# A soft-capped attention with two feed-forward layers: VectorE's order within a pair of heads, the queue of the first queries, and the last copy

## The chip, the cores and the metric

The kernel runs on one core of a Trainium2 chip. A core has five engines with instruction queues of their own: TensorE (PE, with its weight loads shown as PEld), VectorE (DVE), ScalarE (ACT), GpSimd (POOL) and SyncE (SP), which here only starts transfers. They run in parallel and wait for each other through semaphores; within one engine the instructions go in the order in which they were issued. The metric is the device time of one execution in microseconds (us).

## The reference

Attention with a soft cap over 2 batches of 12 heads, 448 tokens and 64 dimensions; its result, laid out as 896 tokens by 768, goes through two feed-forward layers.

```python
scores = scale * np.matmul(q, k.transpose(0, 1, 3, 2))
scores = cap * np.tanh(scores / cap)
scores = scores - np.max(scores, axis=-1, keepdims=True)
attn = np.exp(scores)
attn = attn / (np.sum(attn, axis=-1, keepdims=True) + 1e-09)
x = np.matmul(attn, v)                      # -> 896 x 768
g = s * np.maximum(x @ w_in, 0.0) ** 2 + b  # w_in 768 x 2048
x = g @ w_out                               # 2048 x 768
h = x @ w2_in                               # 768 x 1024
solu = h * softmax(h)
ln = (solu - mean) / np.sqrt(var + 1e-06) * g_ln
out = ln @ w2_out                           # 1024 x 768
```

The weights of the layers are float64 and are converted on the chip.

## The kernel before

**Precision.** Most factors are split into a high and a low part, and a product is three matmuls (high by high, high by low, low by high).

**The attention** runs over 12 pairs of heads. For a pair n, scores are computed by key: TensorE makes four score tiles `s` (`scores_by_key`, L465), ScalarE takes the tanh of each (L470) and then the exponential of two stretches of the tile `e` (`exps_by_key`, L477). The sum over the keys goes through `sums_by_key`: GpSimd adds the first two key tiles of each head (L486, as soon as the first exponential is there), then the third (L489, after the second exponential), and VectorE adds the last piece with two instructions, one for each head (L492, the *last additions* of the sum `c`). Two pairs later TensorE multiplies `e` by the values (`products_by_key`, tile `o`, L504) and sums `c` over the partitions by a matmul with ones (`values_by_key`, tile `m`, L514). VectorE then normalises: a transpose of `m` (`mt`, L521), a reciprocal (`few`, L523), a transpose back (`rs`, L527) and the product `xf` (L532). GpSimd splits `xf` into high and low (`split_x`, L541 and L545), for the last two pairs ScalarE and VectorE do. Meanwhile the keys and queries of pair n+2 are transposed on TensorE (`pk`, `pq`, L423) and split by VectorE and ScalarE (`prep_half`, tiles `kh`, `kl`, `qh`, `ql`, L446, L447, L434 or L438, L439). In the same loop the first weights are converted piece by piece (`weights.pump`, L222 to L247: one instruction or a few in a pair).

**What sets the order.** In the loop over pairs, `then(step, ...)` chains each step behind the one before on TensorE, VectorE, ScalarE and GpSimd, so on each engine the order is the one written in the loop. In a pass n VectorE has: normalisation of n-2, splits of n+2, conversion, last additions of n. The tiles `o`, `m`, `pk` and `pq` share four PSUM banks (`ps_t`), the score tiles have two pairs of banks, `xf` has two buffers, `c` and `e` three.

**The start.** k and q of the first two pairs are loaded into buffers that later hold weights (`raw`, named `first["k"]` and `first["q"]`). SyncE and ScalarE issue the keys of the first pair and, behind them, one head's queries each (L147); GpSimd zeroes the unused parts of the key tiles (L94) and issues the queries of the second pair (L126).

**The end.** The last 128 rows of the result come in two column blocks (512 and 256 wide). Each is copied from PSUM in two halves, the first by ScalarE (L1036), the second by VectorE (L1037), and then stored.

**After the attention** TensorE runs through the two layers; the weights are loaded by SyncE and converted by ScalarE and VectorE ahead of their use.

Of the kernel before, what the change touches and what calls it, by code (L numbers as in the profile page):

```python
# [37 lines left out]
def tile_softcap_attention__relu2__solu(  # L38
# [15 lines left out]
    nc = tc.nc  # L54
# [5 lines left out]
    NC = 4  # L60
# [70 lines left out]
    first = {}  # L131
# [4 lines left out]
    nc.scalar.dma_start(out=cap_t, in_=cap.partition_broadcast(P))  # L136
    ident = cst.tile([P, P], F32, name="ident")
    make_identity(nc, ident)
    zero_by_key(first["k"], True)
    load_by_query(first["q"][:, 1:], q, 0, slice(2, 4), nc.gpsimd)  # L140
    for pr in range(2):
        pair = slice(2 * pr, 2 * pr + 2)
        odd = nc.scalar if pr == 0 else nc.sync
        load_by_key(first["k"][:, pr:pr + 1], k, 0, pair, by_pair=True, odd=odd)
        if pr == 0:
            for j, queue in enumerate((nc.sync, nc.scalar)):
                queue.dma_start(  # L147
                    out=first["q"][:, 0, :, j],
                    in_=q[0, j].rearrange("(p c) d -> p c d", c=NC),
                )  # L150
    s_t = cst.tile([P, 1], F32, name="s_t")
    b_t = cst.tile([P, 1], F32, name="b_t")
    a_t = cst.tile([P, 1], F32, name="a_t")
# [28 lines left out]
    def layers(ctx, general):  # L182
# [229 lines left out]
        st = {}  # L412
# [68 lines left out]
        def sums_by_key(n, half):  # L481
            e = st["e", n]
            if half == 0:
                c = ap_.tile([P, 2, S], F32, tag="c", name=f"c{n}", bufs=3)
                st["c", n] = c
                nc.gpsimd.tensor_tensor(out=c, in0=e[:, 0:2, :], in1=e[:, 2:4, :], op=ALU.add)  # L486
                return
            c = st["c", n]
            nc.gpsimd.tensor_tensor(out=c, in0=c, in1=e[:, 4:6, :], op=ALU.add)  # L489
            for j in range(2):  # L490
                r = slice(j * D, (j + 1) * D)
                nc.vector.scalar_tensor_tensor(  # L492
                    out=c[r, j, :], in0=c[r, j, :], scalar=1e-9 / D, in1=e[r, 6, :],
                    op0=ALU.add, op1=ALU.add,
                )
# [210 lines left out]
        NPR = NH // 2  # L706
# [8 lines left out]
        if general:  # L715
            load_group(2, ("v",))
            for n in range(NPR + 2):
                for c in range(NC):
                    i, c2 = 2 * n + c // 2, c % 2
                    if i < NH:  # L720
                        scores(i, c2)
                    if 0 <= i - 1 < NH:
                        exps(i - 1, c2)
                    if 0 <= i - 2 < NH:
                        transposes(i - 2, 2 * c2)
                        transposes(i - 2, 2 * c2 + 1)
                    if c < 2:
                        prep_half(n + 1)
                if n % 2 == 1 and n // 2 + 3 < NG:
                    load_group(n // 2 + 3)  # L730
                if n >= 2:
                    values(n - 2)
        else:
            last = {}
            traced = nc.cur_bb.bb.instructions

            def then(step, *args):
                with ExitStack() as behind:
                    for ins in last.values():
                        behind.enter_context(tc.issue_after(ins))  # L740
                    n = len(traced)
                    step(*args)
                for ins in traced[n:]:
                    if ins.engine in ordered:
                        last[ins.engine] = ins

            ordered = [e.engine for e in (nc.tensor, nc.vector, nc.scalar, nc.gpsimd)]
            xs["x"] = act_tiles("x")
            idle = ps_t.tile([P, 512], F32, tag="t", name="idle2")
            for n in range(6):  # L750
                nc.tensor.matmul(idle[:D, :D], lhsT=ones, rhs=ones, start=True, stop=True)
            then(scores_by_key, 0, 0)
            then(scores_by_key, 0, 1)
            then(prep_half, 1)
            then(prep_half, 1)
            weights.load(0)
            load_group(2, ("k", "q"))
            load_small()
            load_group(1, ("v",))
            load_group(2, ("v",))  # L760
            weights.load(1)
            steps = {1: 3, **{n: 1 for n in range(3, NPR - 2)}, NPR - 2: 2, NPR - 1: 3}
            for n in range(NPR + 2):
                now = n < NPR
                if now and n > 0:
                    then(scores_by_key, n, 0)
                    then(scores_by_key, n, 1)
                if not now:
                    then(weights.pump, 2)
                if n == 1:  # L770
                    then(prep_half, 2)
                    then(prep_half, 2)
                    then(sums_by_key, 0, 1)
                if n >= 2:
                    then(products_by_key, n - 2, 0)
                    then(products_by_key, n - 2, 1)
                    then(values_by_key, n - 2)
                if now:
                    then(exps_by_key, n, 0)
                if n >= NPR:  # L780
                    then(split_x, n - 2)
                elif n >= 3:
                    then(split_x, n - 3)
                if now:
                    then(sums_by_key, n, 0)
                    then(scores_by_key, n, 2)
                    then(scores_by_key, n, 3)
                    then(exps_by_key, n, 1)
                if n > 0:
                    then(prep_half, n + 2)  # L790
                    then(prep_half, n + 2)
                then(weights.pump, steps.get(n, 0))
                if now and n > 0:
                    then(sums_by_key, n, 1)
                if n == NPR - 1:
                    then(split_x, n - 2)
                if n % 2 == 1 and n // 2 + 3 < NG:
                    load_group(n // 2 + 3, ("k", "q"))
                if n % 2 == 1 and 3 <= (n + 3) // 2 < NG:
                    load_group((n + 3) // 2, ("v",))  # L800
# [203 lines left out]
        def out2(t):  # L1004
            ln = ln_of.pop(t)
            lh = fin2.tile([P, KF2, P], F32R, tag="lh", name=f"lh{t}", bufs=2)
            ll = fin2.tile([P, KF2, P], F32R, tag="ll", name=f"ll{t}", bufs=2)
            with tc.high_priority(offset=200):
                for n in range(2):
                    ps = ps_x.tile([P, 4, P], F32, tag="x", name=f"x{t}_{n}")  # L1010
                    for c in range(4):
                        nc.tensor.transpose(ps[:, c, :], ln[:, n, c * P:(c + 1) * P], ident)
                    split_evac(lh[:, 4 * n:4 * n + 4, :], ll[:, 4 * n:4 * n + 4, :], ps)
            last = t == NTT - 1
            cuts = (slice(0, 512), slice(512, DM)) if last else (slice(0, NO), slice(NO, DM))
            if t == NTT - 2:
                po = ps_h.tile([P, 2, 512], F32, tag="h", name=f"o{t}")
            else:
                po = ps_o.tile([P, 2, 512], F32, tag="o", name=f"o{t}")
            parts = [po[:, 0, :], po[:, 1, :]]  # L1020
            if last:
                parts[1] = ps_h.tile([P, 2, 512], F32, tag="h", name=f"o{t}b")[:, 0, :]
            ot = wt_tile(f"ot{t}")
            order = [(f, n) for f in range(KF2) for n in range(2)]
            if last:
                order.sort(key=lambda fn: fn[1])
            for f, n in order:
                m = cuts[n]
                o = parts[n][:, :m.stop - m.start]
                wh, wl = (w[:, m] for w in w2o_of[f])  # L1030
                nc.tensor.matmul(o, lhsT=lh[:, f, :], rhs=wh, start=(f == 0), stop=False)  # L1031
                nc.tensor.matmul(o, lhsT=lh[:, f, :], rhs=wl, start=False, stop=False)  # L1032
                nc.tensor.matmul(o, lhsT=ll[:, f, :], rhs=wh, start=False, stop=(f == KF2 - 1))  # L1033
                if last and f == KF2 - 1:
                    half = (m.start + m.stop) // 2
                    nc.scalar.copy(out=ot[:, m.start:half], in_=o[:, :half - m.start])  # L1036
                    nc.vector.tensor_copy(ot[:, half:m.stop], o[:, half - m.start:])  # L1037
                    store(ot, t, m)
            if not last:
                nc.scalar.copy(out=ot.rearrange("p (a m) -> p a m", a=2), in_=po[:, :, :NO])  # L1040
                store(ot, t, slice(0, DM))
# [70 lines left out]
```

## Time and profile before

| | |
|---|---|
| median of 3 runs | 475.89 us (475.87 to 476.15) |
| the profiled execution | 475.96 us, of which the span is 474.2 us |
| TensorE busy | 458.5 us (97%) |
| VectorE busy | 358.2 us (76%) |
| ScalarE busy | 273.1 us (58%) |
| GpSimd busy | 92.5 us (20%) |
| TensorE's granted clock | 0.999 of full speed |

The span is the time from the first to the last event of the trace; the profiled execution has 1.8 us around it. The attention takes the first 104 us or so. GpSimd's 92.5 us lie almost all in it, as do VectorE's busiest stretches; behind it VectorE is in reserve most of the time.

### The profile page before, as it was taken

The numbers are of one execution on the slowest core, as the hardware profiler recorded it, in microseconds if no ns is written. First come the engines' busy times: TensorE is split into PE (matmuls) and PEld (weight loads), VectorE is DVE, ScalarE is ACT, GpSimd is POOL, SyncE is SP. The second block draws the span as 40 slices with busy tenths as digits, with TensorE's granted clock in tenths as the row PEclk, the third lists the DMA queues.
The fourth block names the chain that finished last, engine by engine and source line by source line (L and its number), as shares of the span: only waits on it lengthen the run. The fifth ranks groups of instructions, "written<-read, shape, count | busy, mean of one in ns | idle before, by whom it ended". The sixth has DMA issues, their size and how long they took to land.

```text
span 474.2 us, 6582 instructions
## 1 busy us (share of the span) xinstructions
PE 458.5 (97%) x2432; PEld 378.1 (80%) x2432; DVE 358.2 (76%) x566; ACT 273.1 (58%) x394; POOL 92.5 (20%) x91
## 2 busy tenths in 40 slices
PE   7789999999999999999999999999999999999995
PEld 6545465546899898998988889898888898999894
DVE  2799999998798999995699988998959984043110
ACT  3978988781586766755677755555625453033120
POOL 8677777882000000000000000000001010000000
PEclk9999999999999999999999999999999999999999
DMA  7784460014435775532323224443412401011112
GB/s 146 169 198 99 111 180 1 12 56 133 156 115 177 223 218 177 157 117 82 90 80 99 88 91 133 134 133 134 133 68 68 132 1 33 2 33 35 35 45 62
DMA packets 45081, 49.28 MB, mean 104 GB/s; under 512 B 21808, under 2 KB 37296, under 8 KB 45040
## 3 DMA queue, kind: packets, MB, share of 16 engines
q1 hardware_dynamic: 43568, 47.85, 34.8%
q0 software_dynamic: 384, 0.69, 0.7%
q8 instruction: 21, 0.34, 0.3%
q10 hardware_dynamic: 1088, 0.23, 0.2%
q14 instruction: 20, 0.16, 0.1%
HBM read 46.01 MB, written 2.75 MB: 103 GB/s over the span
## 4 chain that ended last, share of the span: by engine, by line
PE 75%; DVE 16%; SPq 4%; DMA 2%; issue 1%; ACT 1%; ACTq 0%; DVEq 0%
PE y L333 8%; PE y L334 8%; PE y L332 8%; PE in L332 7%; PE in L333 7%; PE in L334 7%; DVE c L492 5%; PE h L982 4%; PE h L986 4%; PE h L990 4%; PE o L1032 4%; PE o L1033 4%; PE o L1031 4%; SPq L112 3%; PE o L504 1%
## 5 line engine op out<-in xcount | busy, mean ns | idle before, releaser
L333 PE MATMUL in<-xl,h_wi 128*128 128x510 f32 (+2 forms) x192 | 70.2, 366 | 0.0
L332 PE MATMUL in<-xh,h_wi 128*128 128x510 f32 (+2 forms) x192 | 69.9, 366 | 0.4 <-ACT xh L203 0.4
L334 PE MATMUL in<-xh,l_wi 128*128 128x510 f32 (+2 forms) x192 | 69.9, 365 | 0.0
L967 POOL TENSOR_SCALAR va<-vs 128x1 f32<-128x1 f32 x7 | 2.0, 288 | 321.9 <-ACT e L966 321.9
L364 ACT ACTIVATE gh<-g,s_t 128x510 fp32r<-128x510 f32 (+1 forms) x64 | 42.1, 667 | 18.8 <-PE y L334 18.8
L365 DVE SCALAR_TENSOR_TENSOR gl<-g,s_t,gh 128x510 fp32r<-128x510 f32 (+1 forms) x64 | 42.7, 682 | 3.0 <-ACT gh L364 2.8
L470 ACT ACTIVATE e<-s 128x896 f32<-128x896 f32 (+1 forms) x48 | 36.8, 818 | 11.3 <-PE s L465 11.2
L504 PE MATMUL o<-e,vn 128*64 128x448 f32 x192 | 39.0, 545 | 3.5 <-DVE mt L521 3.5
L477 ACT ACTIVATE e<-e,a_t 128x1792 f32<-128x1792 f32 (+1 forms) x24 | 40.7, 1698 | 0.8
L333 PEld LDWEIGHTS in<-xl,h_wi 128*128 128x128 f32 x192 | 36.0, 188 | 5.3 <-issue 1.4
L332 PEld LDWEIGHTS in<-xh,h_wi 128*128 128x128 f32 x192 | 35.9, 188 | 5.0 <-ACT xh L203 0.7
L334 PEld LDWEIGHTS in<-xh,l_wi 128*128 128x128 f32 x192 | 36.0, 188 | 4.3 <-issue 0.7
L1031 PE MATMUL o<-w2o_h,lh 128*128 128x384 f32 (+1 forms) x104 | 35.6, 342 | 0.5 <-ACT lh L203 0.5
L1033 PE MATMUL o<-w2o_h,ll 128*128 128x384 f32 (+1 forms) x104 | 35.4, 342 | 0.0
L1032 PE MATMUL o<-w2o_l,lh 128*128 128x384 f32 (+1 forms) x104 | 35.4, 340 | 0.0
L492 DVE SCALAR_TENSOR_TENSOR c<-c,e 64x448 f32<-64x448 f32 x24 | 33.1, 1377 | 0.4
L982 PE MATMUL h<-w2i_h,yh 128*128 128x512 f32 x84 | 33.0, 393 | 0.0
L986 PE MATMUL h<-w2i_l,yh 128*128 128x512 f32 x84 | 33.0, 392 | 0.0
L990 PE MATMUL h<-w2i_h,yl 128*128 128x512 f32 x84 | 32.8, 390 | 0.0
L504 PEld LDWEIGHTS o<-e,vn 128*64 128x64 f32 x192 | 13.7, 136 | 23.4 <-issue 16.8
L486 POOL TENSOR_TENSOR c<-e 128x896 f32<-128x896 f32 x12 | 28.9, 2406 | 5.7 <-ACT e L477 5.3
L489 POOL TENSOR_TENSOR c<-c,e 128x896 f32<-128x896 f32 x12 | 25.6, 2130 | 14.2 <-ACT e L477 14.2
(428 smaller groups left out, 1089.4 us busy)
## 6 DMA issues: line engine op xcount, KB each, us to landing
raw<-in_moe_w_in_dram SPq DMA_DIRECT2D x16, 768.0 KB, 4.9
raw<-in_moe_w_out_dram SPq DMA_DIRECT2D x24, 512.0 KB, 3.6
raw_w2i<-in_moe_w_in_dram SPq DMA_DIRECT2D x12, 512.0 KB, 3.7
raw<-in_moe_w_out_dram SPq DMA_DIRECT2D x8, 768.0 KB, 4.3
qn<-in_q_dram SPq DMA_DIRECT2D x16, 112.0 KB, 3.0
vn<-in_v_dram SPq DMA_DIRECT2D x12, 128.0 KB, 2.8
kn<-in_k_dram SPq DMA_DIRECT2D x20, 64.0 KB, 3.4
vn<-in_v_dram SPq DMA_DIRECT2D x12, 96.0 KB, 2.6
```

The source lines that it names most:

```text
L332: nc.tensor.matmul(o, lhsT=wh, rhs=xh, start=first, stop=False)
L333: nc.tensor.matmul(o, lhsT=wh, rhs=xl, start=False, stop=False)
L334: nc.tensor.matmul(o, lhsT=wl, rhs=xh, start=False, stop=last)
L365: nc.vector.scalar_tensor_tensor(out=gl[:, :m], in0=r2, scalar=s_t, in1=full(gh[:, :m]), op0=ALU.mult, op1=ALU.subtract,)
L492: nc.vector.scalar_tensor_tensor(out=c[r, j, :], in0=c[r, j, :], scalar=1e-9 / D, in1=e[r, 6, :], op0=ALU.add, op1=ALU.add,)
L504: nc.tensor.matmul(o[j * D:(j + 1) * D, :S], lhsT=vn[:, 2 * (n % 2) + j, c * D:(c + 1) * D], rhs=st["e", n][:, 2 * c + j if c < 3 else 6, ...
L982: nc.tensor.matmul(ps[:, n, :], lhsT=yh[:, kk, :], rhs=big["w2i_h"][:, kk, f], start=(kk == 0), stop=False,)
L986: nc.tensor.matmul(ps[:, n, :], lhsT=yh[:, kk, :], rhs=big["w2i_l"][:, kk, f], start=False, stop=False,)
L990: nc.tensor.matmul(ps[:, n, :], lhsT=yl[:, kk, :], rhs=big["w2i_h"][:, kk, f], start=False, stop=(kk == KD - 1),)
L1031: nc.tensor.matmul(o, lhsT=lh[:, f, :], rhs=wh, start=(f == 0), stop=False)
L1032: nc.tensor.matmul(o, lhsT=lh[:, f, :], rhs=wl, start=False, stop=False)
L1033: nc.tensor.matmul(o, lhsT=ll[:, f, :], rhs=wh, start=False, stop=(f == KF2 - 1))
```

## The change

Three things are changed.

1. **The last additions.** They are taken out of `sums_by_key` into a step of their own, `ends_by_key(n)`. In the pass for pair n, from n = 2 on, the step stands ahead of the splits of n+2 and does pair n-1; VectorE's order is then normalisation of n-2, last additions of n-1, splits of n+2, conversion. GpSimd's second addition of a pair stays where it was.
2. **The first queries.** All queries of the first pair go to GpSimd's queue, those of the second pair to ScalarE's; SyncE has one transfer less. The zeroing of the first key tiles is written behind the loads.
3. **The last copy.** Each of the two column blocks of the last rows is copied by ScalarE alone.

```diff
-    zero_by_key(first["k"], True)
-    load_by_query(first["q"][:, 1:], q, 0, slice(2, 4), nc.gpsimd)
     for pr in range(2):
...
         if pr == 0:
-            for j, queue in enumerate((nc.sync, nc.scalar)):
-                queue.dma_start(
-                    out=first["q"][:, 0, :, j],
-                    in_=q[0, j].rearrange("(p c) d -> p c d", c=NC),
-                )
+            load_by_query(first["q"][:, :1], q, 0, slice(0, 2), nc.gpsimd)
+            load_by_query(first["q"][:, 1:], q, 0, slice(2, 4), nc.scalar)
+    zero_by_key(first["k"], True)
...
             nc.gpsimd.tensor_tensor(out=c, in0=c, in1=e[:, 4:6, :], op=ALU.add)
+
+        def ends_by_key(n):
+            e, c = st["e", n], st["c", n]
             for j in range(2):
...
                 if n == 1:
                     then(prep_half, 2)
                     then(prep_half, 2)
-                    then(sums_by_key, 0, 1)
+                    then(ends_by_key, 0)
...
+                if 1 < n < NPR:
+                    then(ends_by_key, n - 1)
                 if n > 0:
                     then(prep_half, n + 2)
                     then(prep_half, n + 2)
                 then(weights.pump, steps.get(n, 0))
-                if now and n > 0:
+                if now:
                     then(sums_by_key, n, 1)
+                if n == NPR - 1:
+                    then(ends_by_key, n)
...
-                    half = (m.start + m.stop) // 2
-                    nc.scalar.copy(out=ot[:, m.start:half], in_=o[:, :half - m.start])
-                    nc.vector.tensor_copy(ot[:, half:m.stop], o[:, half - m.start:])
+                    nc.scalar.copy(out=ot[:, m], in_=o)
```

VectorE in the middle of the pair loop, from the splits of one pass to the normalisation and splits of the next (a name's number is only the buffer's running number). Before:

```order
L439 SCALAR_TENSOR_TENSOR ql_527<-pq_521,sc_t,qh_526 128x448
L240 SCALAR_TENSOR_TENSOR wt_wi_357<-raw_58,wt_wi_357 128x768
L492 SCALAR_TENSOR_TENSOR c_496<-c_496,e_456 64x448 x2
L521 STREAM_TRANSPOSE mt_580<-m_577 128x448
L523 RECIPROCAL few_582<-mt_580 128x14
L527 STREAM_TRANSPOSE rs_584<-few_582 128x448
L532 TENSOR_TENSOR xf_586<-o_568,rs_584 128x448
L446 CAST kh_612<-pk_607 128x512
```

The same place after:

```order
L435 SCALAR_TENSOR_TENSOR ql_527<-pq_521,sc_t,qh_526 128x448
L236 SCALAR_TENSOR_TENSOR wt_wi_357<-raw_58,wt_wi_357 128x768
L520 STREAM_TRANSPOSE mt_578<-m_575 128x448
L522 RECIPROCAL few_580<-mt_578 128x14
L526 STREAM_TRANSPOSE rs_582<-few_580 128x448
L531 TENSOR_TENSOR xf_584<-o_566,rs_582 128x448
L491 SCALAR_TENSOR_TENSOR c_494<-c_494,e_454 64x448 x2
L442 CAST kh_612<-pk_607 128x512
```

The two last additions have moved behind the four instructions of the normalisation; the same is so in each of the passes from the third on.

GpSimd at the start of the program (`raw_59` holds the first queries, `raw_58` the first keys). Before:

```order
masks.py:197 MEMSET ident 128x128
L94 MEMSET raw_58 64x2x64 x2
L126 DMA raw_59<-in_q_dram 112x4x64
masks.py:199 ISA
masks.py:199 AFFINE_SELECT ident<-ident 128x128
L126 DMA raw_59<-in_q_dram 112x4x64
```

After:

```order
masks.py:197 MEMSET ident 128x128
L126 DMA raw_59<-in_q_dram 112x4x64 x2
L94 MEMSET raw_58 64x2x64
masks.py:199 ISA
masks.py:199 AFFINE_SELECT ident<-ident 128x128
L94 MEMSET raw_58 64x2x64
```

Both query transfers of GpSimd, now those of the first pair, stand ahead of the zeroing and of the second half of the identity matrix.

The scheduler also moves a few of TensorE's matmuls where the attention ends (the last two sums `m` go behind some of the first layer's matmuls), with the same instructions on both sides, and it moves the loads of one group of values by four places on SyncE's queue.

## Rows read from the trace of the kernel before

**Rows 1.** Waits, 30 to 105 us: engine line waited for, total us, times, longest
```profile
ACT e L470 <- PE s L465: 8.9, 7, 2.2
PE o L504 <- DVE mt L521: 3.5, 5, 1.3
```

**Rows 2.** Timeline of TensorE: start us, us, instruction [idle before, releaser]
```profile
31.29 3.23 PE L504 MATMUL o<-e,vn 128*64 128x448 f32 x16 [1.27 <-DVE mt L521]
...
37.63 0.47 PE L465 MATMUL s<-qh,kh 64*128 64x448 f32 x2
...
42.11 0.92 PE L514 MATMUL m<-c,ones 128*64 128x448 f32 x4
...
45.39 0.47 PE L465 MATMUL s<-qh,kh 64*128 64x448 f32 x2
```

**Rows 3.** Chain that ended last, in order of time: start us, us, what
```profile
29.93 0.62 DVE c L492
...
44.36 2.43 DVE c L492
```

**Rows 4.** Timeline of GpSimd, columns as in Rows 2
```profile
30.06 2.44 POOL L489 TENSOR_TENSOR c<-c,e 128x896 f32<-128x896 f32 x1 [1.50 <-ACT e L477]
...
43.80 2.50 POOL L486 TENSOR_TENSOR c<-e 128x896 f32<-128x896 f32 x1
46.91 2.09 POOL L489 TENSOR_TENSOR c<-c,e 128x896 f32<-128x896 f32 x1 [0.61 <-ACT e L477]
...
49.83 1.16 POOL L545 TENSOR_TENSOR xl<-xf,xh 128x448 fp32r<-128x448 f32 x1
```

**Rows 5.** Groups of instructions, 34 to 92 us: busy us, mean ns | idle before
```profile
L492 DVE SCALAR_TENSOR_TENSOR c<-c,e 64x448 f32<-64x448 f32 x14 | 23.7, 1695 | 0.2
...
L489 POOL TENSOR_TENSOR c<-c,e 128x896 f32<-128x896 f32 x7 | 14.7, 2099 | 10.0 <-ACT e L477 10.0
...
L521 DVE STREAM_TRANSPOSE mt<-m 128x448 f32<-128x448 f32 x7 | 4.6, 651 | 0.2
L532 DVE TENSOR_TENSOR xf<-o,rs 128x448 f32<-128x448 f32 x7 | 4.4, 625 | 0.2
L541 POOL TENSOR_SCALAR xh<-xf 128x448 fp32r<-128x448 f32 x7 | 4.0, 568 | 0.5 <-DVE xf L532 0.5
L240 DVE SCALAR_TENSOR_TENSOR wt_wi<-raw,wt_wi 128x768 uint32<-128x768 uint32 x2 | 1.9, 949 | 0.0
```

**Rows 6.** Timelines of GpSimd, ScalarE, TensorE, VectorE at the start, columns as in Rows 2
```profile
0.98 0.45 POOL L94 MEMSET raw<- 64x128 f32 x2
1.40 0.97 POOL L126 DMA_DIRECT2D raw<-in_q_dram  x1
...
7.84 0.64 ACT L438 ACTIVATE qh<-pq,sc_t 128x448 fp32r<-128x448 f32 x1 [3.22 <-issue]
...
7.17 0.57 PE L423 MATMUL pq<-ident,raw 112*128 112x112 f32 x4 [1.00 <-DMA raw<-in_q_dram]
...
7.00 0.69 DVE L447 TENSOR_TENSOR kl<-pk,kh 128x512 fp32r<-128x512 f32 x1
8.51 0.68 DVE L439 SCALAR_TENSOR_TENSOR ql<-pq,sc_t,qh 128x448 fp32r<-128x448 f32 x1 [0.81 <-ACT qh L438]
```

**Rows 7.** DMA issues of the first 20 us: count, KB each, us from issue to landing
```profile
raw<-in_q_dram POOLq DMA_DIRECT2D x2, 112.0 KB, 4.0
...
raw<-in_q_dram SPq DMA_DIRECT2D x1, 112.0 KB, 4.6
```

**Rows 8.** Timeline of TensorE behind the attention, columns as in Rows 2
```profile
124.49 0.67 PE L332 MATMUL in<-xh,h_wi 128*128 128x448 f32 x2 [0.37 <-ACT xh L203]
```

**Rows 9.** Instructions of lines L1036 and L1037: duration ns min/median/max, first and last start
```profile
L1036 ACT COPY ot<-o x1: 372/372/372, 466.0 to 466.0; 128x256 f32<-128x256 f32 x1
L1036 ACT COPY ot<-o6b x1: 266/266/266, 468.5 to 468.5; 128x128 f32<-128x128 f32 x1
...
L1037 DVE COPY ot<-o6b x1: 292/292/292, 468.8 to 468.8; 128x128 f32<-128x128 f32 x1
```

## The prediction

> **What bounds the kernel now.** I began with the share of each engine and the busy tenths: TensorE is busy nearly throughout, so a gain can only come from its gaps. The list of waits, cut to the pair loop, names them: TensorE waited five times, 3.5 us in all, ahead of the value product `o`, for VectorE's `mt` [rows 1]. The reader is to see that no other long wait of TensorE stands in that stretch, and that ScalarE waits there for TensorE, 8.9 us in seven times, so it has time in hand. The timeline of TensorE then gives the floor of a pair: from the first scores at 37.63 to the next pair's first scores at 45.39 it has no gap, 7.76 us [rows 2]. Where it does stop, it is for a bank: `o` takes the bank of an older `m`, which `mt` frees.
>
> Why is `mt` late? In the chain of work that ended last VectorE stands in unbroken sequence, with the two last additions right ahead of `mt`. One alone takes 0.62 us; the one that began at 44.36 took 2.43 and ended at 46.79 [rows 3]. Beside it GpSimd ran L486 from 43.80 to 46.30, and the addition ended 0.49 behind it [rows 4]: it waited until GpSimd was done and ran then. GpSimd's L486, for its part, took 2.50 where the like-sized L489 takes 2.10 undisturbed [rows 4, 5]. So the two engines take turns, a whole instruction at a time, when VectorE reads two operands from SBUF. Over seven pairs the additions took 23.7 us [rows 5], 3.39 a pair against 1.24 free: 2.15 us of waiting a pair. The normalisation does not pay this: `mt` and `xf` keep their 0.65 and 0.63 us throughout [rows 5], though an L489 ran from 46.91 to 49.00 [rows 4].
>
> The page "SBUF — State Buffer" of the Trainium skill, section "SBUF: two separate sides", says that VectorE and GpSimd share one port pair, locked for a whole instruction, the loser blocked fully; 2.43 against 0.62 agrees.
>
> **The change, part by part.** *The additions behind the normalisation.* No instruction is added or removed in the loop; two are moved past four. `mt` then no longer stands behind the additions: it can start 1.24 us earlier where they ran free and 3 to 4 where they waited. That is more than any of the five stops, the longest of which is 1.27 [rows 2]. Take the first: there the additions ran nearly free, the second at 29.93, so `mt` came some 1.3 us later than it could; moved, it ends at about 29.95 instead of 31.25, and `o`, which TensorE could have begun at 30.02, waits for nothing.
>
> Where do the additions fall now? `m` ends at 43.03 in the pair shown [rows 2]; normalisation takes 0.65 for each of two transposes, 0.63 for the product and about 0.25 for the small reciprocal (an estimate from what the mean durations leave), so 2.2 us [rows 5], to about 45.3. L486 undisturbed would end near 45.9, and L489 begins at 46.91. GpSimd stood idle ahead of L489 for 10.0 us in seven pairs, 1.4 us each [rows 5]; the additions, 1.24 free, arrive near the end of L486 and fit into that gap. VectorE's pair is then 2.2 + 1.24 + 2.0 for three splits out of PSUM (`kl` 0.69, `ql` 0.68 [rows 6], `kh` taken alike) + 0.95 for the longest conversion [rows 5] = 6.4 us, under TensorE's 7.76: TensorE sets the pace and VectorE waits for `m`. ScalarE gives up 3.5 of its 8.9 us.
>
> The moved step brings one wait, for GpSimd's L489 of the pair before, and splits and conversion are queued behind it; that L489 is a whole pass old, so it costs nothing. `xf` gets a wait for GpSimd's split of an older pair (two buffers); that split lies ahead of L486 and L489 of a later pair in GpSimd's queue, so it is past too. Splits of n+2 come 1.24 us or more later in VectorE's queue, but TensorE reads them two passes on.
>
> Bounds: the whole 3.5 and the 0.2 or so of other stops go (−3.7); or nothing goes (0). A part stays in the first passes, where VectorE is behind from its first conversion: after the normalisation of pair 0, near 31.5, the additions of pair 1 meet the L489 that begins at 30.06 [rows 4] and end near 33.4 to 34.0 (a short split of 0.57 [rows 5] may slip between them), while `m` of pair 1 could start at 33.1. That is 0 to 0.9 us of wait; I take 0.5. **Loop: −3.0 us.**
>
> *The end of the loop.* The additions of pair 10 now stand between the normalisation of pair 9 and a run of conversions, which goes on through a weight load to the last `xf` and to `xh`, for which TensorE waits 0.37 us at 124.49 [rows 8]; so 0.37 is the most that can be gained there. If the additions push the conversions by their whole 1.24, that wait grows by as much. I take a value near zero, since the first conversion waits for ScalarE anyway, whose order is kept: **+0.2** (−0.4 to +1.2). The few matmuls that change places there keep TensorE filled either way: 0.
>
> *The first queries.* TensorE could have taken `pq` at 6.17 and waited 1.00 us for the queries of the first pair [rows 6]. GpSimd's first transfer moves to where its zeroing stands, 0.98, and takes 0.97 to issue [rows 6]; the second starts near 1.95. GpSimd's query transfers landed 4.0 us after their issue [rows 7]: near 5.95, ahead of 6.17, so the 1.00 goes. What follows is `qh`, then `ql`, which began at 8.51 but cannot begin ahead of the end of `kl` at 7.69 [rows 6]: 0.82 gets through to the first tanh, and the exponentials behind it run without a pause. Bounds: with SyncE's 4.6 [rows 7] the last part would land near 6.55 (−0.6); landing at 7.2 gives 0. Of the covers, ScalarE's second transfer is hidden by its 3.22 us of idle ahead of `qh` [rows 6]; the zeroing, and with it the identity, moves from 0.98 to behind both transfers, near 2.7, still well ahead of the key transposes that end at 6.17; SyncE's later loads come a transfer earlier. **−0.8 us.**
>
> "DMA: Bandwidth & Descriptors" of the Trainium skill speaks against this part: its table "Specifications" gives the GpSimd path about 1 us to the first byte and SyncE's and ScalarE's about 0.6. The rows have GpSimd's 4.0 against 4.6, its first one having been issued early. By the page a 4.6 becomes an estimated 5.0, `pq` starts near 6.95 and the part gives 0.2.
>
> *The last copy.* Of the last block, ScalarE's 0.266 and VectorE's 0.292 follow each other; ScalarE alone took 0.372 for 256 columns [rows 9]: **−0.2 us**, straight on the path. The wider block is copied 2 us earlier and stays hidden.
>
> Sum: −3.0 + 0.2 − 0.8 − 0.2 = −3.8; from the profiled execution's 475.96 this is 472.16, and 0.07 less from the median of the runs: **472.1 us**.
>
> **Rivals.** *Turns with GpSimd become the bound.* GpSimd's four instructions of a pair need 2.10 + 2.10 + 0.57 + 1.16 [rows 4, 5] = 5.93, the additions 1.24 and a long conversion 0.95: 8.12 us if all take turns, 0.36 above TensorE's 7.76. In five passes with a long conversion that leaves 1.8 us of waits: 473.9. For it: nothing in the order lets two of them overlap. Against: GpSimd may run late by most of a pass before anyone waits for it.
>
> *The first queries land no earlier*, behind the keys on the same transfer engines: the 0.8 is lost, 472.9.
>
> *The wait moves from `o` to `m`*, since the additions that `m` needs have become later: the loop gives nothing, only start and tail count, about 475.0, not to be told from no change.
>
> *Slower: the conversion now meets GpSimd.* Behind the splits it may fall on L486 while the additions go on waiting for L489. Price: half an L486, 1.05 us, in seven passes with a conversion, 7.4 less 1.0 from start and tail: 482.3. It decides from the point where additions and conversion together wait over 2.15 + 0.3 us a pair. Against: the conversion also lies near GpSimd now, and VectorE has 1.4 us in hand.
>
> **How the numbers follow.** Forecast 0.55, turns 0.18, queries 0.12, wait moved 0.08, slower 0.07. The first three are faster: 0.85; 0.2% (0.95 us) is about what a measurement of this kernel can tell from no change, which leaves 0.08 for the same and 0.07 for slower. Low end: −3.7 in the loop, −0.4 behind it, −0.8 and −0.2: 470.8. High end: the rival with the turns and 0.4 more behind the loop, 474.3. The last two rivals stay outside.
>
> **What would show it.** Right: TensorE's wait for `mt` gone from the waits of the loop, pairs near 7.76, additions near 0.62 each, VectorE idle ahead of `mt`; `pq` near 6.2; one copy of 0.37 at the end. Wrong: additions still near 1.7 us on average, a wait of `m` for `c`, or a gap well over 0.37 at the first `xh` of the last pair.

## The result and the profile after

| | before | after |
|---|---|---|
| median | 476.84 us (475.87 to 478.03, 6 runs) | 472.42 us (471.94 to 473.38, 6 runs) |
| ratio after/before | | 0.9919 (0.9901 to 0.9938) |
| profiled execution / its span | 475.96 / 474.2 us | 472.03 / 470.2 us |

The changed kernel is faster by 0.8%, 3.9 us between the profiled executions and 4.4 between the medians. The forecast was 472.1, in a range of 470.8 to 474.3.

The page of the changed kernel, busy time of each engine and the shares of the chain that ended last:

```profile
PE 458.4 (97%) x2432; PEld 376.5 (80%) x2432; DVE 346.0 (74%) x564; ACT 273.3 (58%) x394; POOL 92.1 (20%) x91
...
PE 89%; ACT 3%; DVE 3%; DMA 2%; issue 1%; ACTq 0%; DVEq 0%; SPq 0%
```

In the kernel before, that chain read

```profile
PE 75%; DVE 16%; SPq 4%; DMA 2%; issue 1%; ACT 1%; ACTq 0%; DVEq 0%
```

VectorE's share of it fell from 16% to 3%. TensorE's work is the same to 0.1 us; its stops went.

Waits of the pair loop after, 29 to 104 us (engine, line, what it waited for: total us, times, longest), against [rows 1]:

```profile
POOL c L485 <- ACT e L473: 12.2, 10, 1.8
...
DVE mt L520 <- PE m L513: 7.1, 8, 1.7
ACT e L466 <- PE s L461: 5.7, 6, 1.5
```

No row has a matmul of `o` waiting for `mt` any more; of the weight loads (PEld) one does, 0.3 us in place of 5.7 in six. The wait has turned round: VectorE now waits for `m` ahead of `mt`, 7.1 us. ScalarE's wait for TensorE fell from 8.9 to 5.7, by as much as the loop got shorter (3.2).

Groups of instructions, 34 to 92 us (busy us, mean ns of one | idle before), against [rows 5]:

```profile
L485 POOL TENSOR_TENSOR c<-c,e 128x896 f32<-128x896 f32 x8 | 17.4, 2177 | 10.1 <-ACT e L473 10.1
L491 DVE SCALAR_TENSOR_TENSOR c<-c,e 64x448 f32<-64x448 f32 x16 | 12.1, 755 | 0.3
L540 POOL TENSOR_SCALAR xh<-xf 128x448 fp32r<-128x448 f32 x7 | 5.7, 814 | 0.0
L520 DVE STREAM_TRANSPOSE mt<-m 128x448 f32<-128x448 f32 x8 | 5.2, 648 | 6.6 <-PE m L513 6.6
L531 DVE TENSOR_TENSOR xf<-o,rs 128x448 f32<-128x448 f32 x8 | 5.0, 624 | 0.8
```

One addition takes 755 ns on average in place of 1695. GpSimd now pays a little of it: its `xh` went from 568 ns to 814. It still stands idle for 10.1 us ahead of its second addition, so nobody waits for that.

TensorE in two pairs in the middle of the loop (start us, us, instruction):

```profile
42.77 0.60 PE L419 MATMUL pk<-ident,kn 128*128 128x128 f32 x4
...
50.55 0.60 PE L419 MATMUL pk<-ident,kn 128*128 128x128 f32 x4
...
58.32 0.60 PE L419 MATMUL pk<-ident,kn 128*128 128x128 f32 x4
```

A pair takes 7.78 and 7.77 us, the floor that [rows 2] showed. In the same place VectorE and GpSimd:

```profile
43.63 1.78 DVE L491 SCALAR_TENSOR_TENSOR c<-c,e 64x448 f32<-64x448 f32 x2
45.45 0.69 DVE L442 CAST kh<-pk 128x512 fp32r<-128x512 f32 x1
```

```profile
42.17 2.12 POOL L482 TENSOR_TENSOR c<-e 128x896 f32<-128x896 f32 x1
45.20 2.19 POOL L485 TENSOR_TENSOR c<-c,e 128x896 f32<-128x896 f32 x1 [0.92 <-ACT e L473]
```

The additions come at 43.63, wait for the rest of L482 (it ends at 44.29) and run in GpSimd's gap, to 45.41. The L485 that begins at 45.20, beside their last 0.2 us, takes 2.19 in place of 2.10, and the one at 37.43, beside their last 0.46, takes 2.43: the turns go both ways.

The start, on VectorE, TensorE and ScalarE (first split, first transposes, first tanh), against [rows 6]:

```profile
6.87 0.69 DVE L443 TENSOR_TENSOR kl<-pk,kh 128x512 fp32r<-128x512 f32 x1
7.48 0.67 DVE L435 SCALAR_TENSOR_TENSOR ql<-pq,sc_t,qh 128x448 fp32r<-128x448 f32 x1
```

```profile
5.41 0.63 PE L419 MATMUL pk<-ident,raw 128*128 128x128 f32 x4 [0.85 <-DMA raw<-in_k_dram]
6.12 0.57 PE L419 MATMUL pq<-ident,raw 112*128 112x112 f32 x4
```

```profile
8.93 1.73 ACT L466 ACTIVATE e<-s 128x896 f32<-128x896 f32 x2 [1.51 <-PE s L461]
```

`pq` waits for nothing, `ql` follows `kl`, and the first tanh begins at 8.93 in place of 9.97.

Behind the loop and at the end (TensorE, ScalarE), against [rows 8, 9]:

```profile
120.48 0.68 PE L328 MATMUL in<-xh,h_wi 128*128 128x448 f32 x2 [0.36 <-ACT xh L199]
```

```profile
464.53 0.37 ACT L1038 COPY ot<-o6b 128x256 f32<-128x256 f32 x1 [2.00 <-PE o6b L1036]
```

The wait for the first `xh` is 0.36, as before (0.37). The last copy is one instruction.

### The profile page after: what moved, and what is told of

Its sections match the earlier page's. It is cut to its first block, busy times and chain, and to the rows that moved or that the text cites. A ratio compares the mean times of both kernels' runs of the same rounds, so it can differ in the third digit from the quotient of the medians.

```text
span 470.2 us, 6580 instructions
## 1 busy us (share of the span) xinstructions
PE 458.4 (97%) x2432; PEld 376.5 (80%) x2432; DVE 346.0 (74%) x564; ACT 273.3 (58%) x394; POOL 92.1 (20%) x91
## 4 chain that ended last, share of the span: by engine, by line
PE 89%; ACT 3%; DVE 3%; DMA 2%; issue 1%; ACTq 0%; DVEq 0%; SPq 0%
PE y L330 8%; PE y L328 8%; PE y L329 8%; PE in L328 7%; PE in L329 7%; PE in L330 7%; PE o L503 7%; PE s L461 6%; PE h L985 4%; PE h L989 4%; PE h L993 4%; PE o L1035 4%; PE o L1036 4%; PE o L1034 4%; PE m L513 2%; ACT e L466 2%
## 5 line engine op out<-in xcount | busy, mean ns | idle before, releaser
L1036 PE MATMUL o<-w2o_h,ll 128*128 128x384 f32 (+1 forms) x104 | 35.4, 342 | 0.0
L485 POOL TENSOR_TENSOR c<-c,e 128x896 f32<-128x896 f32 x12 | 26.2, 2187 | 13.2 <-ACT e L473 13.2
L199 ACT CAST lh<-x 128x512 fp32r<-128x512 f32 x14 | 7.5, 590 | 35.7 <-PE o L1035 35.6
L482 POOL TENSOR_TENSOR c<-e 128x896 f32<-128x896 f32 x12 | 25.8, 2152 | 4.0 <-ACT e L473 4.0
```

## The experiments

All ratios are to runs of the kernel before on the same chip. Since executions differ by a microsecond or so, most readings below use three lengths inside a trace: the time of the first tanh; the **loop**, from there to the one late scores matmul that waits some 0.23 us for `e` in every kernel (at 94.08 us before, 89.82 after); and the **end of the loop**, from there to the first `in` matmul of [rows 8]. In us:

| kernel | first tanh | loop | end of the loop |
|---|---|---|---|
| before | 9.97 | 84.11 | 30.41 |
| queries alone | 9.23 | 84.07 | 30.45 |
| copy alone | 10.01 | 84.09 | 30.33 |
| after | 8.93 | 80.89 | 30.66 |
| additions alone | 9.83 | 80.70 | 30.73 |
| after, two store queues | 9.69 | 80.71 | 30.67 |
| after, zeroing first (two executions) | 10.77, 10.38 | 80.70, 81.02 | 30.79, 30.72 |
| before without the additions | 10.46 | 80.24 | 29.26 |
| before, short L486 | 10.48 | 80.25 | 30.28 |
| after, additions behind the splits | 8.97 | 90.02 | 30.83 |
| the same, first pass as in after | 10.20 | 85.25 | 30.61 |

### The additions alone

```diff
+                if 1 < n < NPR:
+                    then(ends_by_key, n - 1)
                 if n > 0:
                     then(prep_half, n + 2)
```

> Only the last additions are moved behind the normalisation; first queries and last copy are as before. Theory (the additions took turns with GpSimd right ahead of mt, and TensorE waited for mt): TensorE's wait ahead of o, 3.5 us in five times before, is gone, the pairs take 7.76 us from the first pass on, the two additions of a pair together take about 1.5 us instead of 3.39. Time 3.0 us (2.7 to 3.5) below before, ratio about 0.9937. Rival (the start brings most of it): under 1.5 us below before.

473.12 us, ratio 0.9919 (0.9897 to 0.9941); profiled span 471.2, 3.0 below before's. Its waits in the loop, 29 to 104 us:

```profile
DVE mt L524 <- PE m L517: 6.7, 7, 1.7
ACT e L470 <- PE s L465: 5.5, 6, 1.4
```

They are close to the waits of the whole change (7.1 and 5.7): the loop's gain is the order's. With the start as before, the loop is 80.70. The ratio is that of the whole change too, 0.9919, so the times by themselves do not tell what the other two parts add.

### The queries alone

```diff
-                for j, queue in enumerate((nc.sync, nc.scalar)):
...
+            load_by_query(first["q"][:, :1], q, 0, slice(0, 2), nc.gpsimd)
+            load_by_query(first["q"][:, 1:], q, 0, slice(2, 4), nc.scalar)
+    zero_by_key(first["k"], True)
```

> Only the queues of the first queries (and the zeroing behind them) are changed. Theory: the query transposes begin near 6.1 us instead of 7.17, the first tanh near 8.95 instead of 9.97, and the whole of this 1.0 us comes through the pair loop: TensorE's wait for mt stays near 3.5 us, the time is 1.0 us below before, ratio 0.998. Rival (VectorE, bound in the loop by its turns with GpSimd, swallows the earlier start): the waits for mt grow by what the start gained, under 0.4 us below before.

475.86 us, ratio 0.9979 (0.9962 to 0.9996); span 473.5. The first tanh is 0.74 earlier, and the waits of TensorE for `mt` in the loop are all there:

```profile
PE o L500 <- DVE mt L517: 3.4, 5, 1.3
```

So in this execution the gain passes through the loop whole (84.07 against 84.11) and stands beside the order's. The interval of the ratio comes close to no change.

### The last copy alone

```diff
-                    half = (m.start + m.stop) // 2
-                    nc.scalar.copy(out=ot[:, m.start:half], in_=o[:, :half - m.start])
-                    nc.vector.tensor_copy(ot[:, half:m.stop], o[:, half - m.start:])
+                    nc.scalar.copy(out=ot[:, m], in_=o)
```

> Only the last copy is in one piece. From the end of the last matmul to the end of the last copy it is 0.37 to 0.40 us instead of 0.61; everything ahead of it is as before. The time is 0.2 us less, below what one execution can tell.

475.95 us in one execution, span 474.2: no difference that can be seen. Inside the trace the copy is there: from the first `in` matmul to the end of the last copy it takes 344.41 us, 344.42 after and 344.63 before. What lies behind the copy, the stores, took 5.08 us before, 5.3 after and 5.36 here, more of a scatter than 0.2.

### The additions left out

```diff
-            for j in range(2):
-                r = slice(j * D, (j + 1) * D)
-                nc.vector.scalar_tensor_tensor(
...
```

> The kernel before without the last additions: the last 64 keys of each head are left out of the sums, so nothing takes VectorE's time right ahead of mt. Theory (the additions are the whole cause of mt's lateness): TensorE's wait for mt is gone, all five times of it; the loop is as short as in the changed kernel, 3.2 us less than before at the end of the attention. Rival (VectorE is late for other reasons too, its conversions beside GpSimd): more than 1 us of waits for mt is left.

471.74 us in one execution, span 469.8. The loop takes 80.24, with VectorE waiting for `m`:

```profile
DVE mt L515 <- PE m L508: 12.8, 9, 2.8
```

So the additions cost the kernel before 3.9 us in the loop, for 1.24 a pair of their own work on an engine with time in hand, and the changed order leaves 0.5 to 0.7 of it. (The loop of this execution began while the granted clock was at 0.50, up to 11 us, so 3.9 is if anything too little.)

### The instruction beside them made shorter

```diff
-                nc.gpsimd.tensor_tensor(out=c, in0=e[:, 0:2, :], in1=e[:, 2:4, :], op=ALU.add)
+                nc.gpsimd.tensor_copy(c, e[:, 0:2, :])
```

> The kernel before with GpSimd's first addition of a pair (L486) replaced by a copy of its first operand, so the second key tiles are left out of the sums; VectorE's instructions and all their places are unchanged. Theory (an addition that falls on L486 is held until it ends): L486 takes about 1.15 us instead of 2.1, the additions that stand beside it shrink by about as much, from a mean of 1.70 us each to 1.1 to 1.3, and TensorE's wait for mt falls from 3.5 us to under 1.5. Rival (the additions are slow by themselves, for their operands or the 64 partitions): they stay at 1.6 to 1.7 us and the wait stays above 3.

472.78 us in one execution; span 470.9. VectorE's order is that of before, yet the loop takes 80.25 and no row has a matmul waiting for `mt`; one weight load does, 0.5 us. Two groups, 34 to 92 us, against [rows 5]:

```profile
L492 DVE SCALAR_TENSOR_TENSOR c<-c,e 64x448 f32<-64x448 f32 x16 | 19.3, 1204 | 0.6 <-POOL c L489 0.3
...
L486 POOL COPY c<-e 128x896 f32<-128x896 f32 x8 | 10.1, 1263 | 0.4 <-ACT e L477 0.4
```

The same GpSimd instruction in the kernel without the additions:

```profile
L486 POOL TENSOR_TENSOR c<-e 128x896 f32<-128x896 f32 x8 | 16.9, 2114 | 1.0 <-ACT e L477 0.6
```

GpSimd's instruction became shorter by 0.85 us (from 2.11 to 1.26), and a pair of additions on VectorE, where nothing was edited, by 0.98 (twice 1695 less 1204 ns). That is the waiting of [rows 3, 4], shown from GpSimd's side. A copy also reads one operand where the addition read two; which of the two, length or operands, did it the run does not tell apart.

### The additions one step further back

```diff
-                if 1 < n < NPR:
-                    then(ends_by_key, n - 1)
                 if n > 0:
                     then(prep_half, n + 2)
                     then(prep_half, n + 2)
+                if 1 < n < NPR:
+                    then(ends_by_key, n - 1)
```

> The changed kernel with the last additions one step further back, behind the splits of the next pair instead of ahead of them. Theory (what counts is where the additions fall beside GpSimd): two microseconds later they meet GpSimd's second addition, which runs there for 2.1 us; the pair of additions takes about 3 us instead of 1.5, VectorE's idle time ahead of mt goes, and TensorE waits again for mt, between 0.3 and 2.5 us in the loop: 0.3 to 2.5 us above the changed kernel. Rival (what counts is only that the additions no longer stand right ahead of mt): additions stay near 0.75 us each, time as the changed kernel within 0.3 us.

480.84 us, ratio 1.0072 (1.0047 to 1.0097): **slower than the kernel before**, and by more than either theory gave. Its waits in the loop:

```profile
PEld m L513 <- DVE c L491: 9.5, 16, 2.2
...
PE m L513 <- DVE c L491: 2.7, 2, 1.5
```

This is the rival "the wait moves from `o` to `m`", and it can cost more than the wait that it takes away. It has two parts. In the first pass that does it VectorE's splits push the additions to 32.37, and they take 3.45: beside them run GpSimd's `xl` (31.78 to 32.93) and L482 (33.03 to 35.33), not the second addition that the theory named. TensorE stops twice:

```profile
33.46 0.97 PE L513 MATMUL m<-c,ones 128*64 128x448 f32 x2 [1.25 <-DVE c L491]
35.88 1.76 PE L513 MATMUL m<-c,ones 128*64 128x448 f32 x2 [1.45 <-DVE c L491]
```

The windows of TensorE there (us: length, busy us and instructions, granted clock, DMA share, GB/s):

```profile
32.00:33.00 1.00, 0.21 (x2) 1.00 0.70 165
33.00:34.00 1.00, 0.54 (x2) 1.00 1.02 347
34.00:35.00 1.00, 0.43 (x2) 1.00 1.15 338
35.00:36.00 1.00, 0.12 (x1) 0.95 1.24 205
36.00:37.00 1.00, 1.00 (x2) 0.50 0.81 118
37.00:38.00 1.00, 1.00 (x3) 0.50 0.05 9
38.00:39.00 1.00, 1.00 (x7) 0.50 0.22 49
39.00:40.00 1.00, 1.00 (x7) 0.84 0.60 137
```

Behind four microseconds that were busy for 0.12 to 0.54 of each, the granted clock stood at 0.50, 1.2 GHz, for three more. From `pk` to `pk` (26.62 to 39.84) this pass took 13.22 us, 5.5 over the floor and 4.8 over the same pass of the changed kernel (26.59 to 34.99, 8.40). The second part is in every later pair: 8.38 us in place of 7.77, without any gap in TensorE's row, since the four `m` matmuls are spread over 1.55 us in place of 0.92 while their weight loads wait for `c` (the PEld row above).

### The same, with the first pass as in the changed kernel

```diff
+                if n == 2:
+                    then(ends_by_key, n - 1)
                 if n > 0:
                     then(prep_half, n + 2)
                     then(prep_half, n + 2)
-                if 1 < n < NPR:
+                if 2 < n < NPR:
                     then(ends_by_key, n - 1)
```

> The kernel with the last additions behind VectorE's splits lost 9.3 us against the changed kernel by the end of the attention loop in its profiled execution. In its trace two parts of that can be told apart: the first pass with a pair before it, where m waited 1.25 and 1.45 us for c, the granted clock then stood at 0.50 for three of the next four microseconds, and a pair took 13.1 us in place of 7.8 (5.3 lost); and every later pair, 8.38 us in place of 7.77, because m's four matmuls took 1.55 us in place of 0.92, the weight load of m waiting for c. This kernel puts the additions ahead of the splits in that first pass alone (as in the changed kernel) and leaves them behind the splits in all later pairs. Theory that both parts are separate: the gap of 1.25 and the low clock are gone, the later pairs still take 8.4 us, and the loss at the end of the loop is 4 us (six to seven pairs at 0.62), so a span near 474.3 and a time near the kernel before's. Rival, that the late additions of one pair start the stall wherever it begins: the stall moves to the next pair with m waiting over 1 us and the clock falling, span near 479. Rival, that the first pass alone sets everything (later pairs fall to 7.8 once it is mended): span near 470.5.

476.66 us, ratio 1.0009 (0.9995 to 1.0024); span 475.7. The gap and the low clock are gone, the granted clock stays at 1.00 from 30 to 48 us, and the pairs still take 8.38 and 8.40:

```profile
33.26 1.54 PE L513 MATMUL m<-c,ones 128*64 128x448 f32 x4
...
41.64 1.57 PE L513 MATMUL m<-c,ones 128*64 128x448 f32 x4
...
50.04 1.56 PE L513 MATMUL m<-c,ones 128*64 128x448 f32 x4
```

The two parts are separate, as the theory said: 85.25 in the loop, 4.4 over after, from the pairs, and 4.8 more with the first pass (in the medians 4.2). The span lies 1.4 above the 474.3 expected because this execution's first tanh was late by 1.3. One place further back in VectorE's order gives away the whole gain of the change.

### The zeroing ahead of the query transfers again

```diff
+    zero_by_key(first["k"], True)
     for pr in range(2):
...
-    zero_by_key(first["k"], True)
```

> The changed kernel with the zeroing of the first key tiles ahead of the query transfers, so that GpSimd issues its two query transfers at the places where it issued two before the change (near 1.4 and 2.7 us); the queues are those of the changed kernel. Theory (GpSimd's transfers land 3.6 to 4.3 us after issue, so the place in its queue decides): the second one lands near 6.7 to 7.0, the query transposes begin there instead of at 6.12, the first tanh comes 0.5 to 0.8 us later than in the changed kernel. Rival (the gain came from taking the queries off the queues of the keys): first tanh within 0.1 us of the changed kernel's 8.93.

473.72 us in one execution; the first tanh at 10.77, 1.84 later than after, and so more than expected. GpSimd's two issues, and TensorE:

```profile
1.40 0.97 POOL L126 DMA_DIRECT2D raw<-in_q_dram  x1
...
2.72 0.73 POOL L126 DMA_DIRECT2D raw<-in_q_dram  x1
```

```profile
6.16 1.08 PE L419 MATMUL pk<-ident,raw 128*128 128x128 f32 x4 [1.05 <-DMA raw<-in_k_dram]
7.47 0.98 PE L419 MATMUL pq<-ident,raw 112*128 112x112 f32 x4 [0.23 <-DMA raw<-in_q_dram]
```

Not only the queries but the keys were late, which the edit does not touch. A second run asks whether they are late each time:

> The changed kernel with the zeroing of the first key tiles put back ahead of GpSimd's query transfers, again and timed. In its one look the first tanh began at 10.77, 1.84 us later than in the changed kernel and 0.8 later than in the kernel before, where 0.5 to 0.8 later than the changed kernel was expected; the first keys were transposed at 6.16 in place of 5.41 (SyncE's six issues took 4.75 us in place of 4.16), and the first queries at 7.47 in place of 6.12. Theory: the place behind the zeros costs the second query transfer on GpSimd's queue its lead (issued at 2.72 in place of about 2.2), which is 0.5 to 1.0 us, and the rest of the 1.84 was the landing of the keys, which differs between executions: the first tanh near 10.0 here, ratio to the kernel before 0.994. Rival, that the order on GpSimd's queue delays the keys too, in every execution: pk at 6.1 again, first tanh near 10.8, ratio 0.9955 or above.

473.87 us, ratio 0.9935 (0.9910 to 0.9960).

```profile
5.83 0.63 PE L419 MATMUL pk<-ident,raw 128*128 128x128 f32 x4 [0.85 <-DMA raw<-in_k_dram]
7.16 0.57 PE L419 MATMUL pq<-ident,raw 112*128 112x112 f32 x4 [0.70 <-DMA raw<-in_q_dram]
```

The keys are not late each time: 5.83 lies within the scatter of the other kernels (5.35 to 6.17), so the rival is not borne out. `pq` at 7.16 is where the kernel before had it, 7.17. A part of that is the keys, 0.4 later than after; for the queries themselves TensorE waits 0.70 us here, 1.00 before and not at all after. The place behind the zeros takes most of their lead. The first tanh came at 10.38 and not near 10.0; the granted clock stood at 0.50 to 0.55 from 8 to 11 us here. The ratio's interval holds the changed kernel's 0.9919 as well; the cost of the zeros is shown in the start of the trace, not in the time.

### The last stores on two queues

```diff
-            for step, n, b, c, p0 in sorted(pieces, reverse=True):
+            for i, (step, n, b, c, p0) in enumerate(sorted(pieces, reverse=True)):
...
-                nc.sync.dma_start(out=rows[c, p0:p0 + step, m], in_=ot[n:n + step, m])
+                (nc.scalar if t == NTT - 1 and i else nc.sync).dma_start(out=rows[c, p0:p0 + step, m], in_=ot[n:n + step, m])
```

> The changed kernel with the stores of the last 128 rows issued from two queues, the second piece of each block by ScalarE behind its copy instead of by SyncE behind the first piece. If SyncE's issue of the pieces one behind the other lies on the path at the end, the last piece starts 0.4 to 0.6 us earlier and the time is 0.3 to 0.6 us below the changed kernel; if the landing of the larger piece ends last, it is the same.

472.31 us, ratio 0.9902 (0.9887 to 0.9917), not to be told from the changed kernel's 0.9919 (0.9901 to 0.9938). From the last copy to the end it took 4.9 us, 0.2 below the lowest of the three above (5.08 to 5.36). Inconclusive, and no version that is shown to beat the changed kernel.

## Why the prediction was right, point by point

**The loop, −3.0: right, measured −3.2** (84.11 to 80.89; −3.4 in the kernel with the order alone). The cause was what [rows 3, 4] were read to say: the additions waited for GpSimd's instruction to end, and `mt` stood behind them. Taking the additions out, shortening L486 and moving the additions each end TensorE's wait for `mt`, and each brings the loop to between 80.2 and 81.0.

The Trainium skill, page "SBUF — State Buffer", section "SBUF: two separate sides", names two kinds of VectorE instruction that need the port pair shared with GpSimd: one with two SBUF inputs, against a GpSimd instruction that reads SBUF, and one in a 2-port performance mode. For the first kind both traces agree: `mt` and `xf`, which read PSUM, kept 648 and 624 ns, while additions of two SBUF operands went from 1695 to 755 with their place. No run here has a GpSimd instruction beside them that reads no SBUF.

The prediction's condition, two operands from SBUF, is too narrow. L223 reads one, takes 0.56 us at 113.78 with GpSimd idle, and was held as well, to 0.42 behind the end of GpSimd's L485:

```profile
99.81 2.25 DVE L223 TENSOR_SCALAR wt_wi<-wt_wi 128x768 f32<-128x768 f32 x1
```

```profile
99.12 2.52 POOL L485 TENSOR_TENSOR c<-c,e 128x896 f32<-128x896 f32 x1 [0.59 <-ACT e L473]
```

Whether L223 ran in such a mode no row shows.

**What is left in the first passes, 0.5: right in size, 0.6.** TensorE shows no gap there, but `m` of pair 1 took 1.53 us in place of 0.92, with weight loads waiting for `c` (two waits, 0.7 us together, in the loop): the mildest form of what the prediction called a sign of being wrong. The additions end at 33.39 in the kernel with the order alone, the low end of the 33.4 to 34.0 forecast, and at 32.50 in the changed kernel, whose first tanh is 0.9 earlier. GpSimd's short split did come between. It is the delay of the experiment one step further back, in one pass only.

**Additions near 0.62 each: wrong.** 755 ns on average; a pair of them waits 0.27 us in the mean, up to 0.86 in that first pass. It cost nothing: VectorE's 6.6 us of idle time ahead of `mt` took it.

**The end of the loop, +0.2: right in size, wrong in its cause.** 0.25 was given back, 0.25 to 0.38 in the five executions with the changed order (after, additions alone, two store queues, zeroing first twice). But it is not the wait for `xh`, which the prediction named (0.37 and 0.36). That wait differs between executions, 0.29 to 0.51, and without it the stretch takes 30.04 us in the kernel before and in those with the queries or the copy alone, and 30.27 to 30.30 in all five. TensorE has no other gap there; its matmuls follow each other a little more slowly. Of the same line before (116 to 124 us) and after (112 to 119.9):

```profile
L334 PE MATMUL in<-xh,l_wi 128*128 128x448 f32 x14 | 5.1, 365 | 0.0
```

```profile
L330 PE MATMUL in<-xh,l_wi 128*128 128x448 f32 x14 | 5.2, 368 | 0.0
```

Behind the last `m` of the attention some 46 `in` matmuls follow without a stop. One begins every 202.6 ns before and every 206.7 after, which makes 0.19 of the 0.25. All five kernels that leave the other instructions of VectorE in their old order have the one figure (202.6 or 202.7), all seven executions with the additions moved the other, with the clock granted at 1.00. It goes with the changed order of TensorE's matmuls there, a term that the prediction put at 0; why is open, and no run here was made for it.

**The first queries, −0.8: right, though one execution cannot show it.** The profiled pair gives −1.04, the pair with the queries alone −0.74, and the timed runs of that kernel −1.0 (−1.8 to −0.2). The first tanh lay at 8.93, 9.23, 8.97, 9.69 and 10.20 in the five executions with the new place, 9.40 in the mean, and at 9.97, 9.83, 10.01, 10.46 and 10.48 in the five with the old, 10.15. That is −0.75, with a scatter of over a microsecond, which came from the first keys (`pk` from 5.35 to 6.17), from the queries and from the clock. The step's two sizes were off and cancelled, which is luck: GpSimd issued its transfers at 1.34 and 2.31, where 0.98 and 1.95 were forecast, and they landed 3.6 us after issue in place of 4.0. It was imprecise in one more place: once `pq` is early, the keys become the last to land, and `kl` itself came 0.13 earlier than the prediction took it, with `ql` close on it.

Against this part the prediction set the table "Specifications" of the Trainium skill's page "DMA: Bandwidth & Descriptors". Its figures are times to the first byte, which no trace here shows; the rows give issue to landing. The delay that the prediction made of them did not come. Of the changed kernel's transfers of the first 12 us (count, KB each, us from issue to landing)

```profile
raw<-in_q_dram POOLq DMA_DIRECT2D x2, 112.0 KB, 3.6
raw<-in_q_dram ACTq DMA_DIRECT2D x2, 112.0 KB, 4.5
```

GpSimd's landed sooner than ScalarE's, and `pq` began at 6.12 where the estimate from the page's figures put it near 6.95. How early GpSimd issues them counted, as the zeroing put ahead shows.

**The last copy, −0.2: right inside the trace** (−0.21 to −0.22 up to the copy's end), and not to be found in the time.

**The total.** Between the two profiled spans the parts add up to −3.2 + 0.25 − 1.04 − 0.21 and +0.2 for the stores, −4.0 where −3.8 was forecast. That the sum came so near is in part luck: the −1.04 of this pair is −0.75 in the mean of five executions each, and the six executions of the kernel before reach from 475.87 to 478.03.

**The rivals.** *Turns become the bound*: GpSimd keeps 10.1 us idle ahead of L485, so no. *The wait moves to `m`*: it needs the additions only one step further back, and then costs 4.4 us in the loop by itself, or 9.1 with the first pass. The prediction gave that case the price of no gain, 475.0, where it came to 476.7 and 480.8; the term that was missed is that `m` waits in every pair, and that a stop can bring the lower clock. *Slower, the conversion meets GpSimd*: conversions do meet it. Five in the loop take 0.3 to 0.4 us longer than undisturbed, the one at 92.50 1.4 and L223 at 99.81 1.7, but no matmul waits for them.

## What to carry to other kernels

Where two engines take turns, the place of a short instruction in the order counts for more than its length: here two additions of 0.62 us cost 3.9 us on an engine that had time in hand, and 0.5 to 0.7 in the gap between two of GpSimd's instructions. Look for the place that is behind what others wait for and ahead of what can wait, and try the neighbouring place too, since one step too late lost all that the change had won, or twice that. A gain at the start of a kernel should be read from several executions, where the first landing scatters more than the gain.

## What the runs showed of the hardware that was not expected

- A stop can cost more than its length: two stops of 1.25 and 1.45 us with little between them were followed by three microseconds of a granted clock of 0.50, and the pass took 5.5 us over the floor. A single stop of 1.27 at the same place in the kernel before [rows 2] left the clock at 1.00.
- At the start the granted clock fell to 0.50 in two of twelve profiled executions (the kernel without the additions, 8 to 11 us; the zeroing first, 9 to 11), and stayed at 1.00 in others with stops of like length: 0.77 and 0.87 us before the one fall, 0.85 and 0.70 before the other, 0.55 and 1.25 in the kernel with the short L486 without a fall. What decides it there is open.
- TensorE can lose 0.6 us a pair without any gap in its row: late weight loads show up as longer matmuls (1.55 us in place of 0.92 for four), and only the list of waits names them, in the rows of PEld.
